# Attention scores with tokens on partitions, and the exponentials turned by block transposes and copies in SBUF

## The chip, the cores and the metric

The kernel runs on one core of one Trainium2 chip. A core has five engines that run side by side, each in its own program order: TensorE (PE, with its weight loads as PEld), VectorE (DVE), ScalarE (ACT), GpSimd (POOL) and SyncE (SP), which here only issues copies. Copies run on 16 DMA engines, fed by queues; a copy issued by SP waits in SP's queue until what it depends on is done, and the copies behind it wait with it. SBUF holds tiles of 128 partitions; PSUM has eight banks of 128 x 512 numbers of 32 bits, into which TensorE writes.

The metric is device time in microseconds (us) for one execution, lower being better.

## The reference

One transformer block over 2048 tokens of width 576. A conditioning vector gives six rows (shift, scale, gate for each half). The first half is attention: 32 query heads over 16 cached key and value heads, with the last 512 keys only and no mask. The second half is a gated ReLU network of width 4608.

```python
W = min(4096, max(256, Sk // 4))                      # 512
q = (x @ wq).reshape(B, Sq, Hq, Dh).transpose(0, 2, 1, 3)
k = jnp.repeat(k_cache[:, :, Sk - W:, :], rep, axis=1)
v = jnp.repeat(v_cache[:, :, Sk - W:, :], rep, axis=1)
scores = jnp.einsum("bhqd,bhkd->bhqk", q, k) * (Dh ** -0.5)
p = softmax(scores, axis=-1)
o = jnp.einsum("bhqk,bhkd->bhqd", p, v)
return o.transpose(0, 2, 1, 3).reshape(B, Sq, Hq * Dh) @ wo
...
h = layernorm(x) * (1 + ca) + sa
x = x + ga * A(h)
h = layernorm(x) * (1 + cb) + sb
x = x + gb * B(h)            # B: (relu(h @ W_gate) * (h @ W_up)) @ W_down
```

## The kernel before

**Numbers in two parts.** TensorE multiplies in a format (F32R) that keeps only part of a 32-bit number. So each operand is split into a high part, a copy in that format (`hi`, made by ScalarE), and a low part, the rest (`lo`, a subtraction on POOL or VectorE). A product is three matmuls: high by high, and the two mixed ones.

**Units.** Attention runs over 128 units; a unit is one head and one block of 512 tokens. Two heads share a key and value head. The loop at the end of the program issues, for each unit u, the scores of u, the projection of the queries of u+1 (`qproj`, 14 matmuls of 512 columns), the values of u-1 (12 matmuls) and two pieces of the output projection (`wo_piece`, 12 matmuls of 288 columns each, adding to the running output `acc`). `run(u, k)` puts further steps at hooks between them: weights to load and split, layer norms, the rearranging of the second half's weights. The order on PE, VectorE, ScalarE and POOL is that of the program text; nothing is reordered afterwards.

**A unit before.** The scores lie with keys on partitions: in `s_half` the keys are the stationary operand, the 512 tokens the moving one (12 matmuls, two halves of 128 x 1024 numbers in PSUM, pool `psS` with two buffers). The maximum over the keys is thus across partitions. It is found by transposing reductions on VectorE (L546), a small reduction (L551), a transpose of 32 x 32 blocks (`turn`, L562), a transpose on TensorE (`spread`, L565) and another reduction (L585), and laid out over the partitions by a transpose of a broadcast (L589). `exp_half` subtracts it on VectorE (L602, PSUM to SBUF) and takes the exponential on ScalarE (L604, 128 x 1024). The sum for the denominator is made like the maximum: additions on VectorE and POOL (`ksum_op`, L619, L622), then L556 and the second half of the small transposes; for the first three units (`by_sum`) TensorE sums with a matrix of ones (`pv_sums`). `hi_half` (L597) and `lo_half` (L611) split the exponentials at the end of unit u; `pv_half` uses them in unit u+1, the first half before and the second half after the exponentials of that unit. `o_mul` (L668) divides by the sum, `o_hi` and `o_lo` split the result.

**Output pieces before.** For most pieces ScalarE copies `acc` into PSUM first (`put_seed`, L720), the matmuls add to it, and ScalarE copies it back (L696); the others are added by VectorE (L698).

**Tiles.** `pp` holds exponentials, high and low parts (three, three and two buffers of 128 x 1024); `psM` has two PSUM buffers of one bank, for projections, small transposes and values in turn; `psW` has one of two banks for the output pieces.

Of the kernel before, what the change touches and what calls it, by code (L numbers as in the profile page):

```python
# [26 lines left out]
SUM, MLP0 = 3, 8  # L27
# [4 lines left out]
def kernel(  # L32
# [22 lines left out]
    pp = ctx.enter_context(tc.tile_pool(name="pp", bufs=3))  # L55
# [4 lines left out]
    sp = ctx.enter_context(tc.tile_pool(name="sp", bufs=2))  # L60
    psS_scope = tc.tile_pool(name="psS", bufs=2, space=bass.MemoryType.PSUM, side="right")
# [17 lines left out]
    mxs = cp.tile([P, 32], F32, name="mxs")  # L79
    nc.vector.memset(mxs, 0.0)  # L80

    zeros = cp.tile([P, 32], F32, name="zeros")
    nc.vector.memset(zeros, 0.0)

    onesr = cp.tile([P, P], F32R, name="onesr")
    nc.vector.tensor_copy(onesr, ones)
# [146 lines left out]
    def prep_kv(d, g, j):  # L233
        st = {}

        def load():
            st["raw"] = rp.tile([P, 640], F32, tag="raw", name=f"rkv{g}_{j}")
            nc.sync.dma_start(st["raw"][:, :512], kv[g, j])

        def cut():  # L240
            d[g] = wp.tile([P, 10, P], F32R, tag="wB", name=f"kv{g}_{j}")
            split(st["raw"][:, :512].rearrange("p (t n) -> p t n", t=4), 512,
                  d[g][:, 0:4, :], d[g][:, 4:8, :])

        return load, cut
# [51 lines left out]
    pend, pend_act = [], []  # L297
# [3 lines left out]
    def flush(q=None):  # L301
        q = pend if q is None else q
        while q:
            q.pop()()

    class LayerNorm:
# [51 lines left out]
        def norm(self, i, by_pool=()):  # L358
            pool, tag, w = self.where[i]
            n = pool.tile([P, w], F32, tag=tag, name=f"xn{self.key}_{self.qb}_{i}",  # L360
                          **({"bufs": 2} if tag == "lo" else {}))
# [18 lines left out]
        def trans(self, ds, pool, tag, tiles=range(4)):  # L380
            nm = f"lt{self.key}_{self.qb}_{ds[0]}"
            if tag == "w":
                flush()
                flush(pend_act)
# [13 lines left out]
        def affine(self, ds, pool, tag, engs):  # L398
# [26 lines left out]
            for j, (d, e) in enumerate(zip(ds, engs)):  # L425
                nm = f"lf{self.key}_{qb}_{d}"
                if len(e) > 3:
                    fs[d] = self.ps[d]
                elif tag == "p":
                    fs[d] = pool.tile([P, 1024], F32, tag="hi" if d % 2 else "p", name=nm)[:, :512]  # L430
                else:
                    fs[d] = pool.tile([P, 512], F32, tag=tag, name=nm)
# [93 lines left out]
    st_, t4, mt, pt, hi_, lo_, bc, rb, rinv, ks_, pvps, done, o, bps = ({} for _ in range(14))  # L526

    def by_sum(u):
        return 0 <= u < SUM

    sums_ps = {}

    def s_half(u, h):
        g, qb, hd = unit(u)
        k = ks[g]
        t = psS.tile([P, 2, 512], F32, tag="s", name=f"s{u}_{h}")
        st_[u, h] = t
        for j in range(2):
            kt = 2 * h + j
            ps = t[:, j, :]  # L540
            nc.tensor.matmul(ps, k[:, kt, :], qhi[u], start=True, stop=False)  # L541
            nc.tensor.matmul(ps, k[:, 4 + kt, :], qhi[u], start=False, stop=False)  # L542
            nc.tensor.matmul(ps, k[:, kt, :], qlo[u], start=False, stop=True)  # L543
        if h == 0:
            t4[u] = sp.tile([P, 4, 16], F32, tag="t4", name=f"t4_{u}", bufs=1)
        nc.vector.tensor_reduce(t4[u][:, 2 * h:2 * h + 2, :].rearrange("p k b -> p (k b)"),  # L546
                                t.rearrange("p k (b j) -> p (k b) j", j=32),
                                axis=AX.X, op=ALU.max, apply_transpose=True)

    def max_pre(u):  # L550
        nc.vector.tensor_reduce(mxs[:, :16], t4.pop(u).rearrange("p k b -> p b k"), axis=AX.X, op=ALU.max)  # L551

    def sum_pre(u):
        if by_sum(u):
            return
        nc.vector.tensor_reduce(mxs[:, 16:], ks_.pop(u).rearrange("p (b j) -> p b j", j=32),  # L556
                                axis=AX.X, op=ALU.add, apply_transpose=True)

    def turn(u):
        bps[u] = psM.tile([P, 512], F32, tag="mm", name=f"qm{u}")  # L560
        mt[u] = sp.tile([P, P], F32, tag="mt", name=f"mt{u}", bufs=1)
        nc.vector.transpose(mt[u].rearrange("p (a b) -> p a b", a=4), mxs[:, None, :].to_broadcast([P, 4, 32]))  # L562

    def spread(u):
        nc.tensor.transpose(bps[u][:, :P], mt.pop(u), ident)  # L565

    def quads(u, k):
        return bps[u][:, :P].rearrange("p (a k b) -> p k b a", a=4, k=2)[:, k]

    def sum_add(u):  # L570
        r = rinv[u] = sp.tile([P, 16], F32, tag="ri", name=f"ri{u}", bufs=1)
        nc.vector.tensor_reduce(r, quads(u + 1, 1), axis=AX.X, op=ALU.add)

    def sum_inv(u):
        nc.vector.reciprocal(rinv[u], rinv[u])

    def sum_bc(u):
        r = rinv.pop(u)
        rb[u] = bp.tile([P, 512], F32, tag="bc", name=f"rb{u}")
        nc.vector.transpose(rb[u].rearrange("p (b j) -> p b j", j=32),  # L580
                            r[:, :, None].to_broadcast([P, 16, 32]))

    def max_bc(u):
        r = sp.tile([P, 16], F32, tag="r", name=f"r{u}", bufs=1)
        nc.vector.tensor_reduce(r, quads(u, 0), axis=AX.X, op=ALU.max)  # L585
        if u > SUM:
            sum_add(u - 1)
        m = bp.tile([P, 512], F32, tag="bc", name=f"mb{u}")
        nc.vector.transpose(m.rearrange("p (b j) -> p b j", j=32),  # L589
                            r[:, :, None].to_broadcast([P, 16, 32]))  # L590
        if u > SUM:
            sum_inv(u - 1)
        bc[u] = m

    def hi_half(u, h):
        hi_[u, h] = pp.tile([P, 2, 512], F32R, tag="hi", name=f"hi{u}_{h}")
        nc.scalar.copy(hi_[u, h], pt[u, h])  # L597

    def exp_half(u, h):
        t = st_.pop((u, h))  # L600
        p = pp.tile([P, 2, 512], F32, tag="p", name=f"p{u}_{h}")
        nc.vector.tensor_tensor(p, t, bc[u][:, None, :].to_broadcast([P, 2, 512]),  # L602
                                op=ALU.subtract)
        nc.scalar.activation(p, p, AF.Exp, bias=0.0, scale=1.0)  # L604
        pt[u, h] = p
        if h == 0 and u:
            hi_half(u, 0)

    def lo_half(u, h):
        lo_[u, h] = pp.tile([P, 2, 512], F32R, tag="lo", name=f"lo{u}_{h}", bufs=2)  # L610
        nc.gpsimd.tensor_sub(lo_[u, h], pt[u, h], hi_[u, h].bitcast(F32))  # L611

    def ksum_op(u, h):
        if by_sum(u):
            return
        p = pt[u, h]
        if h == 0:
            ks_[u] = xp.tile([P, 512], F32, tag="xm", name=f"ks{u}")
            nc.vector.tensor_tensor(ks_[u], p[:, 0, :], p[:, 1, :], op=ALU.add)  # L619
        else:  # L620
            for j in range(2):
                nc.gpsimd.tensor_tensor(ks_[u], ks_[u], p[:, j, :], op=ALU.add)  # L622

    def pv_half(u, h, late=False):
        g, qb, hd = unit(u)
        if h == 0:
            pvps[u] = psM.tile([P, 512], F32, tag="mm", name=f"pv{u}")
        ps, v, a, b = pvps[u], vs[g], hi_[u, h], lo_[u, h]
        for j in range(2):
# [1267 lines left out]
```

## Time and profile before

| | |
|---|---|
| runs shown | 2839.78, 2840.68, 2841.32 us |
| median | 2840.68 us |
| span of the profiled execution, first to last instruction | 2839.2 us |
| mean granted TensorE clock in it | 1.000 |
| DVE, ACT, POOL busy in 1000 to 1200 us | 164.99, 132.44, 173.91 us of 200 |
| mean DMA rate over the span | 145 GB/s |

The time of the profiled execution is its span and a little around it: the median stands 1.5 us over the span. Attention fills the first 1.6 thousand of the 2839 us; the gated network fills the rest.

How to read the profile's rows. A group of instructions reads: line of the program, engine, operation, tile written <- tiles read, shapes, count | busy time in us, mean ns of one | idle time of the engine just before them <- what ended most of it. A row of the timeline reads: start in us, time taken in us, engine, line, operation, tiles, shapes, count, and in brackets the idle time before it with what ended it. A busy PE is pipelined: the next matmul starts before the one before has ended. The chain that ended last follows the work back from the last instruction, at each step to what released it.

### The profile page before, as it was taken

Reading aid. Unit: us, or ns where it says so; the run is one execution under the profiler, and the core shown is the slowest. Engines: PE = TensorE matmul, PEld = TensorE weight load, DVE = VectorE, ACT = ScalarE, POOL = GpSimd, SP = SyncE. Lnnn points to the kernel's source line nnn. Section 1 sums busy time; section 2 is a strip of 40 time slices with the busy share of each in tenths; the row PEclk is TensorE's granted clock in tenths of the full one; section 3 lists DMA queues with packets and bytes.
Section 4 is the critical chain, followed back from the end, with each engine's and each line's share of the span. In section 5 each row is a group of like instructions: output and inputs, shape, how many; then the busy total and the mean of one; then the engine's idle time right before and its main releaser. Section 6 shows DMA issues by size and latency. Waiting matters only on the chain.

```text
span 2839.2 us, 41692 instructions
## 1 busy us (share of the span) xinstructions
PE 2823.0 (99%) x15183; PEld 2457.3 (87%) x15183; DVE 2194.6 (77%) x3220; ACT 1431.0 (50%) x2020; POOL 2206.1 (78%) x1596
## 2 busy tenths in 40 slices
PE   9999999999999999999999999999999999999999
PEld 7888888888888888888888888888888888888888
DVE  8988788888888888777988877787787566666666
ACT  6766666676666666666756433333333222222220
POOL 6878888888898988777788766778888577777773
PEclk9999999999999999999999999999999999999999
DMA  6322122223332223322244465666677844444443
GB/s 248 109 76 97 60 94 95 84 70 109 106 96 85 93 67 132 100 69 86 73 144 136 149 219 203 228 228 232 248 254 281 313 154 155 156 156 154 152 149 136
DMA packets 166876, 411.40 MB, mean 145 GB/s; under 512 B 15728, under 2 KB 62576, under 8 KB 166672
## 3 DMA queue, kind: packets, MB, share of 16 engines
q1 hardware_dynamic: 132768, 287.65, 31.4%
q10 hardware_dynamic: 33904, 121.09, 10.9%
q8 instruction: 120, 1.97, 0.3%
q14 instruction: 84, 0.69, 0.1%
HBM read 276.53 MB, written 160.73 MB: 154 GB/s over the span
## 4 chain that ended last, share of the span: by engine, by line
PE 90%; POOL 4%; DVE 2%; ACT 2%; issue 1%; DMA 1%; ACTq 0%; SPq 0%; POOLq 0%; DVEq 0%
PE gh_P L1163 28%; PE wo L687 12%; PE qps L465 12%; PE md L687 9%; PE mf L771 6%; PE s L543 4%; PE s L542 4%; PE s L541 3%; PE pv L634 3%; PE pv L632 3%; PE pv L631 3%; POOL lo L611 2%; PE gu L1163 1%; POOL ks L622 1%; ACT p L604 1%
## 5 line engine op out<-in xcount | busy, mean ns | idle before, releaser
L611 POOL TENSOR_TENSOR lo<-p,hi 128x1024 fp32r<-128x1024 f32 x256 | 610.1, 2405 | 0.5
L622 POOL TENSOR_TENSOR ks<-ks,p 128x512 f32<-128x512 f32 x250 | 334.5, 1338 | 247.5 <-ACT p L604 203.4
L546 DVE TRANSPOSE_TENSOR_REDUCE t<-s 128x32 f32<-128x1024 f32 x256 | 317.6, 1245 | 137.9 <-PE s L543 125.6
L1163 PE MATMUL gh_P<-hop_B,wop 128*128 128x512 f32 x1470 | 352.9, 390 | 0.6 <-issue 0.6
L1163 PEld LDWEIGHTS gh_P<-hop_B,wop 128*128 128x128 f32 x1470 | 270.0, 188 | 51.2 <-DVE q L1200 0.8
L602 DVE TENSOR_TENSOR p<-s,mb 128x1024 f32<-128x1024 f32 x256 | 299.9, 1209 | 0.3
L465 PE MATMUL qps<-hTa,wA 128*128 128x512 f32 x1176 | 282.6, 391 | 0.7 <-DVE hTa L447 0.3
L1163 PE MATMUL gh_P<-hop_T,wop 128*128 128x512 f32 x1138 | 282.8, 390 | 0.0
L687 PE MATMUL wo<-woga,ohi 128*128 128x288 f32 x1344 | 279.1, 300 | 1.0 <-POOL woga L217 0.5
L604 ACT ACTIVATE p<-p 128x1024 f32<-128x1024 f32 x256 | 270.4, 1056 | 17.4 <-DVE p L602 17.4
L597 ACT CAST hi<-p 128x1024 fp32r<-128x1024 f32 x256 | 268.9, 1051 | 6.9
L465 PEld LDWEIGHTS qps<-hTa,wA 128*128 128x128 f32 x1176 | 220.1, 188 | 47.9 <-DVE hTa L447 0.8
L687 PE MATMUL md<-wogb,hhi 128*128 128x288 f32 x1280 | 257.2, 294 | 0.0
L519 ACT ACTIVATE qhi<-qps 128x512 fp32r<-128x512 f32 x128 | 76.6, 598 | 337.2 <-PE qps L465 337.2
L1163 PEld LDWEIGHTS gh_P<-hop_T,wop 128*128 128x128 f32 x1138 | 208.8, 188 | 39.3
L687 PEld LDWEIGHTS wo<-woga,ohi 128*128 128x128 f32 x1344 | 218.7, 188 | 16.2 <-ACT p L604 0.8
L687 PEld LDWEIGHTS md<-wogb,hhi 128*128 128x128 f32 x1280 | 212.3, 188 | 10.5 <-DVE q L1188 0.2
L698 DVE TENSOR_TENSOR acc<-md,acc 128x576 f32<-128x576 f32 x160 | 120.0, 754 | 107.2 <-PE md L687 106.1
L1163 PE MATMUL gh_P<-hy_T,wop 128*128 128x512 f32 x618 | 200.6, 391 | 0.0
L687 PE MATMUL wo<-woga,olo 128*128 128x288 f32 x672 | 198.8, 296 | 1.2 <-POOL olo L676 1.1
L687 PE MATMUL md<-wogb,hlo 128*128 128x288 f32 x640 | 188.8, 295 | 0.0
L696 ACT COPY acc<-wo 128x576 f32<-128x576 f32 x228 | 145.0, 636 | 55.1 <-PE wo L687 50.5
(322 smaller groups left out, 7279.7 us busy)
## 6 DMA issues: line engine op xcount, KB each, us to landing
wop<-wk_P SPq DMA_DIRECT2D x133, 640.0 KB
wk_P<-wop ACTq DMA_DIRECT2D x119, 640.0 KB
wr<-wlay SPq DMA_DIRECT2D x68, 384.0 KB
againq<-akq SPq DMA_DIRECT2D x22, 640.0 KB
againo<-ako SPq DMA_DIRECT2D x18, 576.0 KB
rogb<-wd SPq DMA_DIRECT2D x36, 288.0 KB
rwA<-wq SPq DMA_DIRECT2D x32, 320.0 KB
roga<-wo SPq DMA_DIRECT2D x32, 288.0 KB
```

Source lines behind the costliest of these rows:

```text
L465: return [lambda i=i, a=a, b=b: nc.tensor.matmul(ps, a, b, start=(i == 0), stop=(i == n - 1)) for i, (a, b) in enumerate(ops)]
L546: nc.vector.tensor_reduce(t4[u][:, 2 * h:2 * h + 2, :].rearrange("p k b -> p (k b)"), t.rearrange("p k (b j) -> p (k b) j", j=32), axis=AX ...
L597: nc.scalar.copy(hi_[u, h], pt[u, h])
L602: nc.vector.tensor_tensor(p, t, bc[u][:, None, :].to_broadcast([P, 2, 512]), op=ALU.subtract)
L604: nc.scalar.activation(p, p, AF.Exp, bias=0.0, scale=1.0)
L611: nc.gpsimd.tensor_sub(lo_[u, h], pt[u, h], hi_[u, h].bitcast(F32))
L622: nc.gpsimd.tensor_tensor(ks_[u], ks_[u], p[:, j, :], op=ALU.add)
L687: nc.tensor.matmul(ps[:, half, :H2], a[:, sl], w[b][:, cs], start=(n == 0 and seed is None), stop=(n == 5), skip_group_check=seed is not None)
L696: nc.scalar.copy(av, ps[:, :, :H2])
L698: nc.vector.tensor_tensor(av, ps[:, :, :H2], av, op=ALU.add)
L771: nc.tensor.matmul(ps[:, j, :H2], x[:, sl], w[:, c:c + H2], start=i == 0, stop=i == 2)
L1163: nc.tensor.matmul(ps, a, c, start=s not in ("P2", "P3") and i == 0, stop=i == len(ops) - 1, skip_group_check=True)
```

## The change

The scores are laid out the other way, tokens on partitions: in `s_half` a slice of 128 tokens is the stationary operand and the 512 keys the moving one. The matmuls are as many and as large. The maximum is then along a row: one reduction per half, with the sign turned. `exp_half` takes four exponentials of 128 x 512 on ScalarE, in place in PSUM, with the turned maximum as a bias of each partition, and gets the sum of each row as a second output.

The value matmuls still need keys on partitions. So `turn_half` transposes blocks of 32 x 32 on VectorE out of PSUM into one tile in SBUF (`T`, one buffer), and `send` moves the blocks between partitions by 16 copies of 32 partitions x 2 KB on SP's queue, into `PT` (two buffers). The keys are loaded in an order that makes these runs contiguous. The row of reciprocal sums goes out to DRAM in pieces of 4 bytes (`sum_row`) and comes back broadcast over the partitions (`sum_bc`).

`hi_half` and `lo_half` of unit u-1 stand behind the exponentials of unit u, and the low part is written over the exponentials themselves in `PT`. Both halves of the values of u-1 stand at the end of unit u, behind both output pieces. `o_mul` moves to the start of the unit after, with its operands in another order of columns. All output pieces are added by VectorE; the second one of a unit takes a buffer of the scores' pool. The transposes on TensorE, the sums by TensorE in the first units, the additions for the sum and the seeding of pieces are gone. The second half of the program takes its buffers from pools (`pl`, `pp`) that are opened once those of attention are closed.

```diff
-            split(st["raw"][:, :512].rearrange("p (t n) -> p t n", t=4), 512,
-                  d[g][:, 0:4, :], d[g][:, 4:8, :])
+            if j:
+                split(raw.rearrange("p (t n) -> p t n", t=4), 512, hi, lo)
+            else:
+                split(raw.rearrange("p (k c n) -> p c k n", k=4, c=4), 512,
+                      *(x.rearrange("p c (k n) -> p c k n", k=4) for x in (hi, lo)))
...
     def s_half(u, h):
+        k = ks[unit(u)[0]]
+        khi, klo = (k[:, x:x + 4, :].rearrange("p t n -> p (t n)") for x in (0, 4))
+        t = st_[u, h] = psS.tile([P, 2, 512], F32, tag="s", name=f"s{u}_{h}")
+        for j in range(2):
+            ps, sl = t[:, j, :], slice((2 * h + j) * P, (2 * h + j + 1) * P)
+            nc.tensor.matmul(ps, qhi[u][:, sl], khi, start=True, stop=False)
+            nc.tensor.matmul(ps, qhi[u][:, sl], klo, start=False, stop=False)
+            nc.tensor.matmul(ps, qlo[u][:, sl], khi, start=False, stop=True)
+        if h == 0:
+            nm[u] = sp.tile([P, 4], F32, tag="nm", name=f"nm{u}")
+            sm[u] = sp.tile([P, 4], F32, tag="sm", name=f"sm{u}")
+        nc.vector.tensor_reduce(nm[u][:, 2 * h:2 * h + 2], t, axis=AX.X, op=ALU.max, negate=True)
+
+    def exp_half(u, h):
+        t = st_[u, h]
+        for j in range(2):
+            i = 2 * h + j
+            nc.scalar.activation(t[:, j, :], t[:, j, :], AF.Exp, bias=nm[u][:, i:i + 1], scale=1.0,
+                                 accum_out=sm[u][:, i:i + 1])
+
+    def turn_half(u, h):
+        if h == 0:
+            tt[u] = tp.tile([P, 4, 4, 4, 32], F32, tag="T", name=f"T{u}")
+        nc.vector.transpose(tt[u][:, :, :, 2 * h:2 * h + 2, :].rearrange("p c k j t -> p j (c k) t"),
+                            st_.pop((u, h)).rearrange("p j (b t) -> p j b t", t=32))
+
+    def send(u):
+        t = tt.pop(u)
+        pt[u] = pa.tile([P, 4, 4, P], F32, tag="PT", name=f"PT{u}")
+        for a in range(4):
+            for c in range(4):
+                nc.sync.dma_start(pt[u][32 * c:32 * c + 32, a].rearrange("p k n -> p (k n)"),
+                                  t[32 * a:32 * a + 32, c].rearrange("p k i t -> p (k i t)"))
+
+    def sum_row(u):
+        r = sp.tile([P, 4], F32, tag="rr", name=f"r{u}")
+        nc.vector.reciprocal(r, sm.pop(u))
+        nc.sync.dma_start(rrow[u].rearrange("i p -> p i"), r)
+
+    def sum_bc(u):
+        rb[u] = bp.tile([P, 512], F32, tag="bc", name=f"rb{u}")
+        nc.sync.dma_start(rb[u], rrow[u].rearrange("i p -> (i p)")[None, :].to_broadcast([P, 512]))
+
+    def part(t, h):
+        return t[:, :, 2 * h:2 * h + 2, :].rearrange("p a k n -> p k a n")
+
+    def hi_half(u, h):
+        hi_[u, h] = pa.tile([P, 2, 4, P], F32R, tag="hi", name=f"hi{u}_{h}")
+        nc.scalar.copy(hi_[u, h], part(pt[u], h))
+
+    def lo_half(u, h):
+        nc.gpsimd.tensor_sub(part(pt[u].bitcast(F32R), h), part(pt[u], h), hi_[u, h].bitcast(F32))
+
+    def pv_half(u, h):
...
+            hi = a[:, j].rearrange("p a n -> p (a n)")
+            nc.tensor.matmul(ps, v[:, kt, :], hi, start=(kt == 0), stop=False)
+            nc.tensor.matmul(ps, v[:, 4 + kt, :], hi, start=False, stop=False)
+            nc.tensor.matmul(ps, v[:, kt, :], b[:, :, kt, :], start=False, stop=(kt == 3))
...
     def o_mul(u):
         o[u] = rb.pop(u)
-        nc.vector.tensor_tensor(o[u], done.pop(u), o[u], op=ALU.mult)
+        t = o[u].rearrange("p (i a t) -> p a i t", i=4, a=4)
+        nc.vector.tensor_tensor(t, done.pop(u).rearrange("p (a i t) -> p a i t", a=4, i=4), t, op=ALU.mult)
```

The order within a unit, after the change:

```python
    for u in range(NU):
        last = u + 1 == NU
        run(u, 0)
        if u > 1:
            o_mul(u - 2)
        s_half(u, 0)
        s_half(u, 1)
        if u > 1:
            o_hi(u - 2)
            o_lo(u - 2)
        if u:
            sum_bc(u - 1)
        run(u, 1)
        if not last:
            qproj(u + 1, 0, 14)
        run(u, 2)
        exp_half(u, 0)
        turn_half(u, 0)
        exp_half(u, 1)
        turn_half(u, 1)
        send(u)
        sum_row(u)
        if u > 1:
            hi_half(u - 1, 0)
            lo_half(u - 1, 0)
        if not last:
            q_hi(u + 1)
            q_lo(u + 1)
...
        if u:
            hi_half(u - 1, 1)
            lo_half(u - 1, 1)
        run(u, 3)
        todo = pieces(u)
        if todo:
            pend.append(wo_piece(*todo[0]))
        run(u, 4)
        run(u, 5)
        flush()
        run(u, 6)
...
        if todo:
            pend.append(wo_piece(*todo[1], pool=(psS, "s")))
        run(u, 7)
        if u:
            pv_half(u - 1, 0)
            pv_half(u - 1, 1)
        flush()
        run(u, 8)
        run(u, 9)
```

More of the change, by code (lines that the diff above doesn't have):

```diff
@@ L538, in s_half @@
+    def pv_half(u, h):
+        if h == 0:
+            pvps[u] = psM.tile([P, 512], F32, tag="mm", name=f"pv{u}")
+        ps, v, a, b = pvps[u], vs[unit(u)[0]], hi_.pop((u, h)), pt[u].bitcast(F32R)
         for j in range(2):
             kt = 2 * h + j
[L540 to L543, printed above, removed]
@@ L559, in turn @@
[L559 to L572, printed above, removed]
@@ L609, in lo_half @@
[L609 to L622, printed above, removed]
@@ L1807 @@
[L1807 to L1826 removed]
+        run(u, 2)
```

301 lines of the change are left out of this document (75 added, 226 removed).

## The prediction

> **What bounds the kernel now.** I read the page first: its head, part 1 (busy time) and part 4 (the chain that ended last).
>
> ```profile
> span 2839.2 us, 41692 instructions
> PE 2823.0 (99%) x15183; PEld 2457.3 (87%) x15183; DVE 2194.6 (77%) x3220; ACT 1431.0 (50%) x2020; POOL 2206.1 (78%) x1596
> PE 90%; POOL 4%; DVE 2%; ACT 2%; issue 1%; DMA 1%; ACTq 0%; SPq 0%; POOLq 0%; DVEq 0%
> ```
>
> TensorE (PE) bounds it, and the others have slack only on average. So the question is not how much work leaves VectorE (DVE) and GpSimd (POOL), but whether the operands still reach TensorE in time within one unit. For that I read the timeline: first score matmul of the first unit, of three neighbours, and the other TensorE groups of a unit; the "wo" group as the chain in order of time shows it.
>
> ```profile
> 23.61 0.50 PE L541 MATMUL s<-qhi,kv 128*128 128x512 f32 x1 [0.69 <-ACT qhi L519]
> ...
> 985.06 0.39 PE L541 MATMUL s<-qhi,kv 128*128 128x512 f32 x1
> ...
> 997.03 0.39 PE L541 MATMUL s<-qhi,kv 128*128 128x512 f32 x1
> ...
> 999.77 3.35 PE L465 MATMUL qps<-hTa,wA 128*128 128x512 f32 x14
> 1002.95 0.27 PE L565 MATMUL qm<-ident,mt 128*128 128x128 f32 x1
> ...
> 1008.98 0.39 PE L541 MATMUL s<-qhi,kv 128*128 128x512 f32 x1
> ...
> 1568.27 0.39 PE L541 MATMUL s<-qhi,againk 128*128 128x512 f32 x1
> 991.26 1.59 PE wo L687 x12
> ```
>
> The first column is the start, the second the time taken. A unit takes 11.97 and 11.95 us here, and the 127 steps from 23.61 to 1568.27 average 12.163. Fourteen matmuls of 512 take 3.35 us, the last of them 0.39, so one is issued every (3.35 - 0.39)/13 = 0.228 us. TensorE's own work per unit is 12 scores + 14 projections + 12 values = 38 x 0.228 = 8.66, and two pieces of 1.59: 11.84 us. The remaining 0.1 is the small transpose L565. So attention has no gap to win, except that transpose.
>
> **The change, part by part: what leaves TensorE.** L565 goes: 0.1 us x 128 = 13 us at most. The three first units lose 8 sum matmuls each: 24 x 0.228 = 5.5 us. Scores, projections, values and pieces keep their counts and sizes. If nothing waits, that is 18 us less.
>
> **What TensorE must wait for.** Before, hi and lo of unit u are made at the end of unit u. After, both are put behind the four exponentials of unit u+1 in ScalarE's (ACT) queue, and TensorE uses them at the end of the same unit u+1. Engines run in order, so a path from the scores of one unit, through the queues, to the values of the unit before now lies inside one unit. Its rows, from the page's groups and the groups by shape, and two POOL instructions on end in the timeline:
>
> ```profile
> L546 DVE TRANSPOSE_TENSOR_REDUCE t<-s 128x32 f32<-128x1024 f32 x256 | 317.6, 1245 | 137.9 <-PE s L543 125.6
> L597 ACT CAST hi<-p 128x1024 fp32r<-128x1024 f32 x256 | 268.9, 1051 | 6.9
> L519 ACT ACTIVATE qhi<-qps 128x512 fp32r<-128x512 f32 x128 | 76.6, 598 | 337.2 <-PE qps L465 337.2
> L439 ACT ACTIVATE lta<-lta,mcol,mcol 128x512 f32<-128x512 f32 x5 | 3.7, 749 | 3.0 <-PE lta L395 2.1 <-DVE t L546 0.9
> L101 ACT ACTIVATE sT<-cT 128x5 f32<-128x5 f32 x1 | 0.2, 209 | 0.4 <-DMA cT<-c 0.4
> L611 POOL TENSOR_TENSOR lo<-p,hi 128x1024 fp32r<-128x1024 f32 x256 | 610.1, 2405 | 0.5
> 1571.38 4.76 POOL L611 TENSOR_TENSOR lo<-p,hi 128x1024 fp32r<-128x1024 f32 x2
> 1014.91 0.27 PE L565 MATMUL qm<-ident,mt 128*128 128x128 f32 x1
> 1015.22 0.22 DVE L585 TENSOR_REDUCE r<-qm 128x16 f32<-128x64 f32 x1 [0.77 <-PE qm L565]
> ```
>
> One hand-over costs 1015.22 - 1015.18 = 0.04 us. Zero is the first score matmul:
> - scores of the first half end: 5 x 0.228 + 0.39 = 1.53
> - maximum: 0.04 + 1.245 (nearest row L546, same source) = 2.82
> - four exponentials of 512 elements, e us each: 2.86 + 4e
> - hi of the first half of the unit before, behind them: + 1.05 (L597)
> - two lo on POOL: 0.04 + 4.76
> - TensorE needs the second lo at its fourth matmul from the end: 0.04 + 4 x 0.228 = 0.95, then the next unit begins.
>
> The sum is 9.66 + 4e. TensorE itself would reach that matmul 11.84 - 0.91 = 10.93 into the unit; it waits wherever 4e is over 2.2 us.
>
> The trace has no exponential of 512 with a per-partition bias, in place in PSUM, with a sum as second output. L519 (598 ns, constants only) bounds it below: two instructions on end overlap, so a pitch of about 0.6. L439 (749 ns, in place in PSUM, two per-partition operands) is the nearest row; if the sum takes an instruction of its own as small as L101 (209 ns), the end is 0.96. I take 0.78, next to L439, since the sum's output must cost something and one pointer less something back. The period is then 12.78 us. With 0.6 the second maximum decides instead (scores 2.90, maximum to 4.19, two exponentials to 5.43): 12.23. With 0.96 it is 13.50.
>
> The Trainium skill, "ScalarE: Activation LUTs", section "What ACT_TABLE_LOAD costs", gives about 280 ns + 0.833 ns per element with a pointer bias and an overlap of about 93 ns on end. Its constants-only form, 186 ns + 0.833 ns, comes to 0.61 us where L519 has 0.598, so the trace agrees there. The estimate for one exponential on end is then 0.61 us and the period 12.23, which still waits; the section prices no sum output, and no run here shows one yet.
>
> **The sum.** The first nine units (139.32 - 23.61 = 115.7 us by the tenth start, below) hold start-up and norms; without pieces their TensorE work is short and the path counts there too: 9.8 + 8 x 12.78 + some 6 for norms = 118, so +2.
>
> ```profile
> 139.32 0.39 PE L541 MATMUL s<-qhi,againk 128*128 128x512 f32 x1
> L376 ACT ACTIVATE xna<-acc,rsa 128x512 f32<-128x512 f32 x8 | 6.5, 806 | 0.0
> L376 ACT ACTIVATE xta<-acc,rsa 128x128 f32<-128x128 f32 x6 | 2.9, 482 | 0.0
> ```
>
> The other 118 steps take 127 x 12.163 - 115.7 = 1429 us now, 19 of them extra TensorE work, which the wait would swallow. After: 118 x 12.78 = 1508, so +79. In a dozen units norm work (0.81 + 0.48 us per tile) stands in ScalarE's queue ahead of the exponentials, with only some 1.3 us of idle time (from o's high part, done near 1.5, to 2.86) to hide it; I put down 15 us, between 0 and 30. At the end the last values wait for the copies and for both lo with little else to issue: +4 (0 to 10). Together 79 + 2 + 15 + 4 = +100. The runs shown have a median of 2840.68, 1.5 over the profiled span: 2839.2 + 1.5 + 100 = **2941 us**.
>
> **What costs nothing, and its cover.** VectorE gains two maxima, two transposes and two additions (mostly ScalarE copies before), and loses both subtractions, three small transposes, the add for the sum and the reductions. POOL loses two sum additions. Both end with less work, so only order counts. The turn of the first half ends near 2.86 + 1.56 + 0.04 + 1.25 = 5.7; a second piece takes that score buffer at 7.5: 1.8 us of cover. One transpose should lie between L580 (0.70 for half the size) and L546 (1.245), two between 1.4 and 2.5; off the path at either end. Behind ACT's added wait stand q's high part (done near 7.6, wanted by the next scores at 12.8) and the second hi (8.6, wanted by POOL at 9.4); behind POOL's lo stand weight lows and o's low part, wanted by a piece six us into the next unit. Strided reads in hi, lo and the value matmuls, lo in place and the permuted multiply I take at their rows before; a tenth more or less on the lo pair alone moves the period by 0.5 us, and no row excludes it.
>
> Copies: 16 per unit on SyncE's queue (SP), then the two for the row of sums (512 pieces of 4 bytes out, a broadcast row back, used one unit later: a unit of cover), with the weight loads queued behind the first one's wait for the turn.
>
> ```profile
> L580 DVE STREAM_TRANSPOSE rb<-ri x128: 699/701/712, 47.0 to 1594.0; 128x512 f32<-128x512 f32 x128
> 1428.15 0.81 SPq L486 DMA_DIRECT2D againo<-ako  x2
> 1429.06 0.38 SPq L881 DMA_DIRECT2D hk_B<-hy_B  x1
> 350.56 0.58 SPq L1573 DMA_DIRECT2D wlay<-wg  x1
> 1007.00 0.34 SPq L254 DMA_DIRECT2D roga<-wo  x1
> 1008.70 1.56 DVE L262 TENSOR_TENSOR roga<-roga,mrow 128x576 f32<-128x576 f32 x1
> ```
>
> An issue takes 0.4 us on end; a load issued at 1007.00 was used at 1008.70, so 1.7 us to landing at most. The single turned tile is busy for 2.5 (two turns) + 16 x 0.4 + 1.7 = 10.6 us, under the period, and the turned copy lands some 3 us before its hi. The loads behind have a unit of lead. So nothing, as long as an issue stays under 0.53 us.
>
> **The rivals.**
> - *No wait, and faster.* The path must come in under 11.84. It decides at 4e = 2.2 and a second maximum that doesn't bind, or a lo pair 0.4 us cheaper than 4.76. Then only TensorE's relief is left: 2841 - 18 = 2823. Against it: even the cheapest exponential gives 12.23.
> - *The turned tile binds.* At the 0.58 us that a DRAM-to-DRAM copy (L1573) takes to issue, the tile's loop is 2.5 + 9.3 + 1.7 = 13.5: +164 + 21, 3026. For it: the queue is also held by waiting loads; against: the sends are plain copies.
> - *Lo in place holds its neighbour.* If the two halves, interleaved in one tile, are ordered as if they overlapped, hi of the second half waits for the first lo (9.45), the second lo ends at 13.0, and ten value matmuls follow: 15.3 per unit, +376 + 20, 3237. No row shows halves interleaved like this.
>
> **How the numbers follow.** Chances: the path as summed 0.70 (2876 at e = 0.6, as 118 x 12.23 - 1429 + 21 = +35; 3026 at 0.96), turned tile 0.10, lo in place 0.07, no wait 0.09, within 0.2% 0.04. About 0.2%, 6 us, is what a measurement can tell from no change. The range, 2845 to 3060, takes the first case with both ends of e, a little beyond for norms and tail, and most of the second; left out are the faster case and the 3237. Faster 0.09, same 0.04, slower 0.87.
>
> **What would show it.** Right: TensorE idle 0.5 to 1.5 us in each unit ahead of a values matmul that reads lo, released by POOL lo; score starts 12.2 to 13.5 us apart; POOL idle until ACT hi, ACT's hi directly behind the exponentials; DVE and POOL less busy. Wrong: starts 11.85 apart; or VectorE's transposes waiting for a DMA (turned tile); or ACT's second hi waiting for POOL lo (in place). The exponential's mean time tells the size of e.

## The result, and the profile after

The changed kernel takes 4377.10 us (median; 4372.76 to 4379.74) where the kernel before takes 2840.83 (2839.78 to 2841.32): a ratio of 1.541 (1.539 to 1.543), +1536 us. The forecast was slower, but by 100 us, and the time lies far outside its range. First the page of the changed kernel: span, busy time, the chain that ended last by engine and by line, and the packets.

```profile
span 4375.8 us, 44794 instructions
PE 3171.4 (72%) x15030; PEld 2722.4 (62%) x15030; DVE 1933.5 (44%) x2427; ACT 1270.2 (29%) x2332; POOL 1872.9 (43%) x1346
DMA packets 351221, 579.79 MB, mean 132 GB/s; under 512 B 118128, under 2 KB 164976, under 8 KB 350992
DMA 44%; PE 31%; SPq 20%; issue 2%; POOL 1%; ACT 1%; DVE 0%; ACTq 0%; DVEq 0%; POOLq 0%
DMA rr<-r 20%; SPq L566 18%; PE gh_P L1064 18%; DMA rb<-rr 9%; PE md L624 6%; DMA wlay<-wu 5%; DMA wlay<-wg 4%; PE mf L672 4%; DMA PT<-T 1%; POOL PT L586 1%; PE wo L624 1%; DMA againq<-akq 1%; SPq L240 1%; DMA akq<-wA 1%; DMA againo<-ako 1%
```

Every compute engine has slack, TensorE too. The chain, 90% TensorE before, is now 44% DMA and 20% SyncE's queue (SPq). Its lines are the row of sums written to DRAM (rr<-r), the issue of the sixteen copies (L566), the row read back (rb<-rr), and two transfers that the change did not touch: wlay<-wu and wlay<-wg, which lay out the gate and up weights anew in DRAM. Then the waits (waiting engine and line, what it waited for; total us, times, longest), with SyncE's own queue last.

```profile
PE wo L624 <- DVE T L558: 897.4, 120, 23.0
DVE rb L605 <- DMA rb<-rr: 842.4, 109, 14.1
DVE T L558 <- DMA PT<-T: 560.7, 101, 13.2
ACT hi L583 <- DMA PT<-T: 414.7, 110, 26.4
SPq L576 <- DMA rr<-r: 796.9, 114, 9.8
```

TensorE waits for a score buffer (wo piece, L624), VectorE's turn holds that buffer, and the turn waits for the copies of the turn before. So the single turned tile binds, the rival to which I gave 0.10, and with far longer copies than it assumed. The timeline of SyncE's queue shows two units (start, time taken, line, transfer, count).

```profile
1499.83 0.53 SPq L572 DMA_DIRECT2D rr<-r  x1
1500.40 0.64 SPq L1467 DMA_DIRECT2D wlay<-wu  x1
1501.14 4.30 SPq L261 DMA_DIRECT2D roga<-wo  x1
1510.89 0.33 SPq L576 DMA_DIRECT2D rb<-rr  x1
1511.27 0.62 SPq L1467 DMA_DIRECT2D wlay<-wu  x1
1511.98 18.36 SPq L566 DMA_DIRECT2D PT<-T  x16
1530.44 0.53 SPq L572 DMA_DIRECT2D rr<-r  x1
1531.02 0.53 SPq L980 DMA_DIRECT2D wa_P<-wlay  x1
1531.59 0.66 SPq L1467 DMA_DIRECT2D wlay<-wg  x1
1532.35 9.79 SPq L261 DMA_DIRECT2D roga<-wo  x1
1542.23 0.46 SPq L576 DMA_DIRECT2D rb<-rr  x1
```

The unit is the queue: 30.6 us from the row of 1499.83 to that of 1530.44, a long one. A weight load (roga<-wo) that issues in 0.34 us in the kernel before takes 4.30 and 9.79 behind the row; the read-back (L576) begins 11 us after the row's write; the sixteen copies take 18.36 us. Attention runs from the first to the last of these score matmuls of a unit:

```profile
24.31 0.50 PE L540 MATMUL s<-kv,qhi 128*128 128x512 f32 x1 [0.69 <-ACT qhi L523]
3066.96 0.39 PE L540 MATMUL s<-againk,qhi 128*128 128x512 f32 x1
```

That is 3042.7 us, 24.0 per step, against 1544.7 before (23.61 to 1568.27): +1498 of the +1536. The rest lies behind the last unit.

### The profile page after: what moved, and what is told of

It reads as the page before. It is cut to its first block, busy times and chain, and to the rows that moved or that the text cites. A ratio compares the mean times of both kernels' runs of the same rounds, so it can differ in the third digit from the quotient of the medians.

```text
span 4375.8 us, 44794 instructions
## 1 busy us (share of the span) xinstructions
PE 3171.4 (72%) x15030; PEld 2722.4 (62%) x15030; DVE 1933.5 (44%) x2427; ACT 1270.2 (29%) x2332; POOL 1872.9 (43%) x1346
## 2 busy tenths in 40 slices
DMA packets 351221, 579.79 MB, mean 132 GB/s; under 512 B 118128, under 2 KB 164976, under 8 KB 350992
## 4 chain that ended last, share of the span: by engine, by line
DMA 44%; PE 31%; SPq 20%; issue 2%; POOL 1%; ACT 1%; DVE 0%; ACTq 0%; DVEq 0%; POOLq 0%
DMA rr<-r 20%; SPq L566 18%; PE gh_P L1064 18%; DMA rb<-rr 9%; PE md L624 6%; DMA wlay<-wu 5%; DMA wlay<-wg 4%; PE mf L672 4%; DMA PT<-T 1%; POOL PT L586 1%; PE wo L624 1%; DMA againq<-akq 1%; SPq L240 1%; DMA akq<-wA 1%; DMA againo<-ako 1%
## 5 line engine op out<-in xcount | busy, mean ns | idle before, releaser
L586 POOL TENSOR_TENSOR PT<-PT,hi 128x1024 fp32r<-128x1024 f32 x256 | 604.1, 2382 | 913.8 <-ACT hi L583 902.8
L624 PE MATMUL wo<-woga,ohi 128*128 128x288 f32 x1344 | 392.0, 388 | 736.6 <-DVE T L558 631.4
L624 PEld LDWEIGHTS wo<-woga,ohi 128*128 128x128 f32 x1344 | 303.7, 262 | 773.2 <-DVE T L558 652.4
L558 DVE STREAM_TRANSPOSE T<-s 128x1024 f32<-128x1024 f32 x256 | 305.0, 1229 | 725.6 <-DMA PT<-T 560.7
L613 POOL TENSOR_TENSOR olo<-rb,ohi 128x512 fp32r<-128x512 f32 x128 | 162.6, 1270 | 612.6 <-ACT ohi L609 609.8
L583 ACT CAST hi<-PT 128x1024 fp32r<-128x1024 f32 x256 | 266.1, 1041 | 447.5 <-DMA PT<-T 414.7
L624 PE MATMUL wo<-againo,ohi 128*128 128x288 f32 x576 | 165.0, 382 | 305.3 <-DVE T L558 266.0
L552 ACT ACTIVATE s<-s,nm 128x512 f32<-128x512 f32 x512 | 337.4, 659 | 76.0 <-DVE nm L546 64.9
L609 ACT CAST ohi<-rb 128x512 fp32r<-128x512 f32 x128 | 79.1, 618 | 897.2 <-DVE rb L605 897.2
L624 PEld LDWEIGHTS wo<-againo,ohi 128*128 128x128 f32 x576 | 127.0, 256 | 322.5 <-DVE T L558 275.7
L546 DVE TENSOR_REDUCE nm<-s 128x2 f32<-128x1024 f32 x256 | 301.1, 1215 | 13.6 <-PE s L542 13.6
L624 PE MATMUL wo<-woga,olo 128*128 128x288 f32 x672 | 256.7, 382 | 21.9 <-POOL olo L613 21.9
L624 PE MATMUL md<-wogb,hhi 128*128 128x288 f32 x1280 | 257.2, 295 | 0.0
L630 DVE TENSOR_TENSOR acc<-wo,acc 128x576 f32<-128x576 f32 x256 | 191.3, 750 | 111.6 <-PE wo L624 111.5
L624 PEld LDWEIGHTS md<-wogb,hhi 128*128 128x128 f32 x1280 | 212.3, 188 | 10.5 <-DVE q L1089 0.2
```

The lines of the kernel that those rows point to most:

```text
L546: nc.vector.tensor_reduce(nm[u][:, 2 * h:2 * h + 2], t, axis=AX.X, op=ALU.max, negate=True)
L552: nc.scalar.activation(t[:, j, :], t[:, j, :], AF.Exp, bias=nm[u][:, i:i + 1], scale=1.0, accum_out=sm[u][:, i:i + 1])
L558: nc.vector.transpose(tt[u][:, :, :, 2 * h:2 * h + 2, :].rearrange("p c k j t -> p j (c k) t"), st_.pop((u, h)).rearrange("p j (b t) -> p ...
L583: nc.scalar.copy(hi_[u, h], part(pt[u], h))
L586: nc.gpsimd.tensor_sub(part(pt[u].bitcast(F32R), h), part(pt[u], h), hi_[u, h].bitcast(F32))
L613: nc.gpsimd.tensor_sub(olo[u], o.pop(u), ohi[u].bitcast(F32))
```

## The experiments

Each kernel ran beside the kernel before on the same chip (2839.7 to 2840.3 us), with one profile and one time. The effects are tens to hundreds of microseconds. "Sends" are the sixteen copies of a unit.

### Taking the row of sums away, or its pieces

**row_once** writes the row for the first unit only and lets every unit read that one back.

```diff
-        nc.sync.dma_start(rrow[u].rearrange("i p -> p i"), r)
+        if u == 0:
+            nc.sync.dma_start(rrow[0].rearrange("i p -> p i"), r)
```

> The row of reciprocal sums is written to DRAM for the first unit only and every unit reads that one back, so the denominators are left out of the result from the second unit on; the 16 copies, the broadcast and all orders stay. Theory (SyncE's queue is the loop): the row's 512 pieces of 4 bytes hold the queue and the rings for some 10 us a unit (issued at 1499.83, its reader released at 1510.89); without them the loop is two turns 2.4 + 16 issues of 0.63 + about 2 to landing = 14.5 us a unit in place of 22.4: about 128 x 7.9 = 1010 us less, 3370. Rival (the path from scores to the low part, as forecast, is what fills the unit): nothing of it is touched, 4377. Rival (moving 1 MB between partitions is what is slow): sends stay as long as they are, 18 us a unit, about 4000 or more.

Measured 3480.12 us, 897 less than the changed kernel and 110 above the theory's 3370. The pages count the pieces; this one's row of packets:

```profile
DMA packets 284162, 579.49 MB, mean 167 GB/s; under 512 B 51072, under 2 KB 97920, under 8 KB 283936
```

118128 - 51072 = 67056 packets fewer, 127 rows of 528 (512 pieces and 16 that I take for the completion signals), with 0.3 MB between them. So the row costs by its number of pieces or by the wait of its reader, not by bytes. I held that it is the reader (L576), which waits at the head of SyncE's queue with the sends behind it; the rival was the pieces. **bc_late** moves the reader behind the sends:

```diff
-        if u:
-            sum_bc(u - 1)
         run(u, 1)
...
         send(u)
+        if u:
+            sum_bc(u - 1)
         sum_row(u)
```

> The read-back of the row of unit u-1 is issued behind the 16 copies of unit u, not ahead of them; nothing is left out. Theory (the copies stand in the queue behind a wait for the row): the wait is over by then, so 14.5 to 16 us a unit, 3350 to 3560. Rival (the pieces stall the DMA rings themselves, whoever waits): the copies' issue stays blocked, over 20 us a unit, 4100 or more.

4305.07 us: only 72 less. The reader's wait was the longest in the queue's list, 797 us, and moving it explains next to nothing: it still comes to 363 us here, and the queue stalls all the same. My theory of that moment fell. **row16** keeps row and reader, but writes 128 pieces of 16 bytes:

```diff
-        nc.sync.dma_start(rrow[u].rearrange("i p -> p i"), r)
+        nc.sync.dma_start(rrow[u], r)
```

> The whole change with the right result, but the row of sums goes to DRAM as 128 pieces of 16 bytes instead of 512 pieces of 4 bytes; the permutation is done where the output is multiplied (the output's two halves then come from PSUM by ScalarE and VectorE). If the number of pieces sets the stall of the queue (512 pieces about 10 us behind them, 128 about 2.5 us), the unit falls to about 17.5 to 19 us, 3550 to 3730 us, near the 3480 of row_once. Rival: the stall belongs to a write and a dependent read through DRAM as such, whatever the pieces: it stays at 22 us per unit, 4250 to 4400.

3606.92 us, 770 less, with nothing left out. The same edit makes o's high part (ScalarE) and low part (now VectorE) straight from the product in PSUM, and what that alone costs was not run. A quarter of the pieces leaves 3607 - 3480 = 127 of the 897 us, so the pieces are the cost. **before_plus_row** adds the write alone, without a reader, to the kernel before:

```diff
         turn(u)
+        nc.sync.dma_start(xrow[u].rearrange("i p -> p i"), mhalf)
```

> The kernel before, with the same DRAM write of 512 pieces of 4 bytes added to SyncE's queue once a unit and nobody reading it. If the pieces stall whatever comes behind them in the DMA rings for 10 us, weight loads come late and the time rises: by 50 to 500 us. If only a waiting reader makes them dear, the time stays within 10 us of 2841.

3142.88 us, +302: the pieces alone slow a kernel that doesn't use them, 2.4 us per row on average. Nothing holds these writes to one per unit, so the queue runs ahead of the units. In one place it issues eighteen on end, and ScalarE, which issues copies on a queue of its own, stands idle for 33 us:

```profile
1312.63 50.75 SPq L1778 DMA_DIRECT2D xr<-mhalf  x18
1351.84 1.04 ACT L597 CAST hi<-p 128x1024 fp32r<-128x1024 f32 x1 [33.12 <-DMA xr<-mhalf]
```

Two steps there take 42 and 59 us and lose 77 between them, a quarter of the 302. The last row is issued at 1424.6 us, and the last 37 steps take as long as in the kernel before.

**norm** needs no row: VectorE multiplies the exponentials by the reciprocal sums in PSUM, ahead of the turn.

```diff
+        nc.vector.reciprocal(r, sm[u][:, 2 * h:2 * h + 2])
+        nc.vector.tensor_tensor(st_[u, h], st_[u, h], r[:, :, None].to_broadcast([P, 2, 512]), op=ALU.mult)
```

> Nothing is left out: VectorE multiplies the exponentials in PSUM by the reciprocal sums before the turn (two multiplications of 128 x 1024, about 1.2 us each), so no row goes through DRAM, and o is split from PSUM (the low part on VectorE). Theory (the queue is the loop): as without the row's pieces, 14.5 us a unit plus up to 2.4 for the multiplications inside the turned tile's loop or its queue: 3370 to 3680. Rival (path of the forecast): 12.8 to 13.5 a unit, 3060 to 3150. Rival (data of the copies): about 4000.

3540.07 us, 837 less than the changed kernel, with nothing left out.

### The path alone

**path_only** is row_once with the sends of the first two units only; later units read those two tiles again. All compute instructions and their order stay.

```diff
+        if u > 1:
+            pt[u] = pts[u % 2]
+            return
```

> Leaves out: the row of sums of all units but the first, and the copies of the turned tile of all units but the first two; later units read the two tiles of the first two again (their turned data is not computed with). All of TensorE's, VectorE's, ScalarE's and GpSimd's instructions and their order stay. So only the forecast path is left: scores, maximum, four exponentials, hi, lo, values. Theory (the path inside a unit was summed rightly and DMA alone made the rest): score starts 12.8 us apart, as forecast with e = 0.78, about 2940 us, between 2876 (12.23) and 3026 (13.50). Rival (the engines' queues hold more than that path: lo in place, the strided reads, a second maximum): 14 us or more per unit, 3090 or over. If it is at 11.9 per unit, 2823, no path binds at all.

3020.63 us. One unit in the timeline, TensorE's, ScalarE's and GpSimd's rows together:

```profile
1453.50 0.61 PE L540 MATMUL s<-againk,qhi 128*128 128x512 f32 x1
1465.53 0.50 PE L601 MATMUL pv<-PT,againv 128*128 128x512 f32 x1 [0.68 <-POOL PT L590]
1466.57 0.40 PE L540 MATMUL s<-againk,qhi 128*128 128x512 f32 x1
1469.47 0.66 ACT L552 ACTIVATE s<-s,nm 128x512 f32<-128x512 f32 x1 [1.30 <-DVE nm L546]
1470.05 0.19 ACT L552 ACTIVATION_READ_ACCUMULATOR s<-s,nm 128x1 f32 x1
1472.34 0.19 ACT L552 ACTIVATION_READ_ACCUMULATOR s<-s,nm 128x1 f32 x1
1472.44 1.04 ACT L587 CAST hi<-PT 128x1024 fp32r<-128x1024 f32 x1
1473.55 4.75 POOL L590 TENSOR_TENSOR PT<-PT,hi 128x1024 fp32r<-128x1024 f32 x2 [4.01 <-ACT hi L587]
1473.86 1.05 ACT L587 CAST hi<-PT 128x1024 fp32r<-128x1024 f32 x1
24.33 0.50 PE L540 MATMUL s<-kv,qhi 128*128 128x512 f32 x1 [0.69 <-ACT qhi L523]
191.74 0.40 PE L540 MATMUL s<-againk,qhi 128*128 128x512 f32 x1
1740.75 0.40 PE L540 MATMUL s<-againk,qhi 128*128 128x512 f32 x1
```

From 1466.57 the first exponential starts 2.90 us in (forecast 2.86), hi 5.87 (5.98), lo 6.98 (7.07), and TensorE's wait for lo stands where it was forecast, ahead of a values matmul that reads lo (L601). The median of the 127 steps is 12.83 us; 12.78 was forecast. The last three rows of the fence start the first, the tenth and the last unit. **path_hi_first** moves hi and lo of the first half ahead of the exponentials:

```diff
+        if u > 1:
+            hi_half(u - 1, 0)
+            lo_half(u - 1, 0)
         exp_half(u, 0)
```

> path_only (3021 us; leaves out the copies after the second unit and the rows after the first) with hi and lo of the first half of the unit before put ahead of the four exponentials instead of behind them. If the order in ScalarE's queue makes the 12.83 us of path_only, the first lo starts at 2.6 us instead of 7 and the second ends near 10.1, ahead of the 10.93 at which TensorE wants it: 11.85 to 12.0 us per unit, 2870 to 2920 us. Rival (lo on GpSimd is late because of its other work, weight lows and o's low part, whatever the order): 12.5 or more, 2980 or over.

2898.56 us. Two neighbouring units of it:

```profile
1208.86 0.40 PE L540 MATMUL s<-againk,qhi 128*128 128x512 f32 x1
1220.76 0.40 PE L540 MATMUL s<-againk,qhi 128*128 128x512 f32 x1
```

11.90 us, TensorE's own pace. The order on ScalarE's queue made the 12.83 us. Of the 58 us that are left over the kernel before, 48 lie in the first nine steps (163.5 us against 115.7), where the copies of two units and one row still run; the other 118 steps take 5 us more than before. So 2899 is no floor of this order, and where it would stand without any copy isn't shown.

### What the sends cost

**row_once_split** is row_once with every second send issued from ScalarE's queue, behind its hi.

```diff
-                nc.sync.dma_start(pt[u][32 * c:32 * c + 32, a]...
+                if c % 2 != act:
+                    continue
+                (nc.scalar if act else nc.sync).dma_start(pt[u][32 * c:32 * c + 32, a]...
```

> Leaves out the row of sums of all units but the first, as row_once does (3480 us, median unit 15.8 us), and issues the 16 copies from two queues: eight from SyncE where they were, eight from ScalarE behind its hi of the same unit. Theory: what the copies cost is the loop of the single turned tile, two turns 2.5 us, sixteen issues of 0.63 us, 2 us to landing, 14.6 us, and with eight issues per queue it is 9.5 us, under the path; so the unit falls to the path's 12.8 to 13.3 us, 3010 to 3100 us, near path_only's 3021, which has no copies at all. Rival (the copies cost by the traffic that they bring, or by the wait for their landing): 15 us or more per unit, 3350 or over.

3343.47 us: between the theory and the rival. Its trace has the hint: units of 16.8 us on average as long as layout copies (wlay) still leave the queue, and runs of units of 12.8 after the last of them (median there 13.4). So two kernels leave out 132 of those 152 copies:

```diff
+        if i >= len(lay0):
+            continue
         step("lay", ...
```

**split_nolay** on two queues, **one_nolay** on one.

> row_once_split (3343 us, leaves out the row of sums after the first unit) without the copies that lay out the gate and up weights anew in DRAM (132 of the 152 on SyncE's queue during attention, 512-byte packets; their readers take the first two blocks instead, so the gate and up weights of the later feature tiles are not the right ones). If those copies and the sends hold each other on SyncE's queue, the units up to the 88th fall from 16.8 us to those after it, 12.8 to 13.3: 3000 to 3080 us, near path_only's 3021. Rival (the sends themselves are slow while any load runs): 15 us or more per unit, 3250 or over.

> row_once (3480 us, 16 sends on one queue) without the same layout copies. Then the loop of the single turned tile is left: two turns 2.5 us, 16 issues of 0.63 us = 10.1, 2.0 to landing, 14.6 us per unit, as row_once has it after its 88th unit: 118 units of 1.8 us over the path's 12.83 more than path_only's 3021, 3190 to 3260 us. If it is near split_nolay, the issue of the sends is not the bound; if it stays above 3350, other loads hold the queue too.

3049.51 us on two queues, and 3259.51 on one, at the upper end of its range. Now the loop of the turned tile is seen bare; first one_nolay, VectorE's turns and SyncE's sends:

```profile
1011.65 2.38 DVE L558 STREAM_TRANSPOSE T<-s 128x1024 f32<-128x1024 f32 x2 [4.20 <-DMA PT<-T]
1014.09 10.02 SPq L566 DMA_DIRECT2D PT<-T  x16
1025.73 2.38 DVE L558 STREAM_TRANSPOSE T<-s 128x1024 f32<-128x1024 f32 x2 [2.56 <-DMA PT<-T]
L566 SPq DMA_DIRECT2D PT<-T x2048: 507/588/2181, 36.2 to 1992.8; - x187
```

2.44 us from the turns' start to the first issue, 10.02 of issues, 1.62 to landing: 14.08 us in this unit, 14.85 as the median of all steps, above the path's 12.83. Then split_nolay, where SyncE and ScalarE issue side by side:

```profile
1009.20 4.96 SPq L569 DMA_DIRECT2D PT<-T  x8
1009.76 5.36 ACTq L569 DMA_DIRECT2D PT<-T  x7
1014.69 0.40 PE L540 MATMUL s<-kv,qhi 128*128 128x512 f32 x1
1027.52 0.39 PE L540 MATMUL s<-kv,qhi 128*128 128x512 f32 x1
```

Half the issues per queue, and the unit is back on the path: 12.83. The Trainium skill, "DMA: Bandwidth & Descriptors", section "Issuing engines are not separate DMA queues", says that a second issuing engine saves only the sequencer's time to initiate, usually small beside the transfer. The trace agrees on what is saved and not on its size: here the issue is 10.02 us and the landing 1.62, and the second queue saves 3259.5 - 3049.5 = 210 us.

### Versions meant to mend the change

These leave nothing out. **norm_split2** is norm on two queues; **norm_via** is norm with the turned tile written to DRAM in one DMA and read back in four; **row16_split** is row16 on two queues; **row16_split_hi** has hi first as well.

> The kernel norm (VectorE normalises the exponentials, no row through DRAM) with the 16 copies of the turned tile issued from two queues: eight from SyncE where they were, eight from ScalarE behind its hi of the same unit. Theory: the single turned tile's loop (turns and multiplications 3.7 to 5 us, 16 issues of 0.63 us = 10 us, landing 2 us) is the unit of norm (median 16.5 us); with eight issues per queue it falls to 11 to 12 us, so the forecast path binds: 12.8 to 14 us per unit, 2945 to 3100 us. Rival: the copies are limited by what the DMA rings can take of them, not by the issuing queue: still 16 to 17 us per unit, 3500.

> The kernel norm with the move between partitions made through DRAM: the turned tile is written out in one DMA (512 packets of 2048 bytes) and read back in four, five issues instead of sixteen. Theory (the number of issues on SyncE's queue prices the copies): the turned tile is busy for 4 to 5 us of turns, under 1 us of issue and 4 to 5 us of writing, under 11 us, so the unit falls to 12.8 to 14 us, 2945 to 3100 us. Rival (bytes or the landing of 1 MB each way price them): 16 us or more per unit, 3450 or over.

> The whole change, both causes mended as far as they go: the row of sums in 128 pieces of 16 bytes, and the copies on two queues, with the right result. Theory: SyncE's queue then holds 8 issues (5 us), a stall of about 2.5 us and loads of 2 us, 9.5 us, under the path of 12.8, so 12.9 to 13.8 us per unit, 3020 to 3150 us. Rival: the rings stay full behind the pieces on either queue: 15 us or more, 3350 or over.

> row16_split, whole and with the right result, with hi and lo of the first half of the unit before ahead of the exponentials. The turned copy must land by about 1.5 us into the next unit for that: the turn ends near 8, ScalarE issues its eight by 13 to 14, they land by 15 to 16, 3 us into the next unit, so hi first makes the exponentials wait 1 to 2 us for the copy: 12.5 to 13.5 us per unit, 2960 to 3100 us. If the copies land in time, 11.9 to 12.2 and 2880 to 2940. If worse than row16_split, the landing of the copies has become the wait.

Measured 3441.98, 3430.19, 3491.57 and 3539.35 us: all four missed on the slow side. In norm_split2 VectorE's turn waits little for the copies (58 us in all, 459 in row_once); two neighbouring units show a longer path instead:

```profile
1510.41 2.35 DVE L545 TENSOR_REDUCE nm<-s 128x2 f32<-128x1024 f32 x2
1513.54 1.23 DVE L557 TENSOR_TENSOR s<-s,r 128x1024 f32<-128x1024 f32 x1
1514.81 1.25 DVE L560 STREAM_TRANSPOSE T<-s 128x1024 f32<-128x1024 f32 x1
1517.40 1.25 DVE L560 STREAM_TRANSPOSE T<-s 128x1024 f32<-128x1024 f32 x1
1518.68 5.01 ACTq L571 DMA_DIRECT2D PT<-T  x8
1521.96 0.39 PE L599 MATMUL pv<-PT,kv 128*128 128x512 f32 x1
1525.31 0.58 ACT L607 CAST ohi<-pv 128x512 fp32r<-128x512 f32 x1
1525.92 0.69 DVE L609 TENSOR_TENSOR olo<-pv,ohi 128x512 fp32r<-128x512 f32 x1 [5.37 <-ACT ohi L607]
1526.53 2.35 DVE L545 TENSOR_REDUCE nm<-s 128x2 f32<-128x1024 f32 x2
```

From maximum to maximum 16.12 us. The first turn ends at 1516.06, behind its reciprocal and multiplication (1.4 us), and only then is the score buffer free for a piece on TensorE, behind which stand the values and the next scores. The next maximum stands on VectorE behind o's low part (L609), which waits 5.37 us for o's high part on ScalarE (L607). The values end at 1522.35, but ScalarE makes the high part only at 1525.31, because the eight sends that it now issues, two other issues and two copies stand ahead of it. Over all units it starts 2.8 us after the values (median). So the second queue frees SyncE and lengthens the path through ScalarE. In norm_via the read from DRAM lands too late for hi (a wait of ScalarE on it of 349.5 us in all). In row16_split the layout copies were still there, and a median step near 13.9 us behind the last of them, down from 18.3 on average, says that they are part of it. VectorE also waits 374 us in all for the row's read-back (rb<-rr); how the rest divides was not tried. Hi first (row16_split_hi) loses 48 us against row16_split, and ScalarE's hi now waits 258 us in all for DMA. The profile puts that wait down to the row's write (rr<-r), which is issued right behind the sends and which hi doesn't read, so that the landing of the sends has become the wait is my reading. No version tried beats the kernel before.

## Why the prediction was wrong, point by point

**Where the 1536 us lie.** By what was taken away, in this order: path_only stands 180 us above the kernel before; the sends on one queue add 239 (one_nolay, 3260); the layout copies in that queue 221 (row_once, 3480); the row of sums 897 (4377). The parts depend on one another, so another order would divide them otherwise. The step of 239 is not a clean one: path_only still has the layout copies and one_nolay doesn't.

**What bounds the kernel and what leaves TensorE** was right: where nothing waits, path_hi_first runs at 11.90 us per unit, and 11.84 was forecast.

**The path inside a unit** was right in mechanism and size: 12.83 us against 12.78. The exponential's e, taken as 0.78, comes to (1472.44 - 1469.47)/4 = 0.74 here. It is an activation of 0.66 and a read of the sum of 0.19, the guess behind the upper bound; the two overlap a little, which keeps it under 0.78. That the sum is off by 0.05 only is partly luck: the four exponentials came out 0.15 us under, and hand-overs, maximum and the end of the path 0.2 over.

**Start-up and norms** were too small. In path_only the first nine steps (24.33 to 191.74) take 167 us, not 115.7 + 2: +52 where the forecast had +2, part of it the DMAs that this kernel still has in its first units (the second to the fourth step take 74.5 us, 38.6 before). The other 118 take 1549 instead of 1508 + 15, and the tail adds 7 where 4 was forecast. So the path with all its ends is worth 180 at most, not 100: inside the range (3021 against 3060); the 80 us too few are 6% of the miss.

**The copies at nothing** was the first step that failed. "An issue takes 0.4 us on end" came from loads of DRAM into SBUF; a copy from SBUF to SBUF takes 0.59 and follows the next by 0.63. My own bound, nothing as long as an issue stays under 0.53 us, was thus crossed. The rival that I priced at 0.58 us (13.5 per unit, 3026) is the right mechanism, and 14.08 to 14.85 is what it measured bare. The nearest row, a DRAM-to-DRAM copy of 0.58, stood in the prediction itself; I called the sends "plain copies" and gave it 0.10.

**"The loads behind have a unit of lead"** was the second. I asked whether the loads could wait for the sends, and not whether the sends could wait for the loads: 132 layout copies share the queue and cost the turned tile 221 us.

**The row of sums with "a unit of cover"** was the third, and the largest. Cover was counted for its reader; the row's price falls on the copies that come behind it. "512 pieces of 4 bytes" stood in the prediction as a description and carried no price, and no rival had it. The Trainium skill, "DMA: Bandwidth & Descriptors", section "Rules for kernel authors", says that a transfer whose last dimension isn't contiguous becomes one descriptor per element; the packet count above agrees, and row_once and row16 give the price.

**The rivals.** No wait fell: TensorE waits for lo even without any copy. Lo in place fell: path_only has both halves in place, and the two lo follow each other in 4.75 us, and hi of the second half (1473.86) runs beside the first lo instead of waiting for it.

## What to carry to other kernels

Price a moved step on its queue, not only on its engine: for every DMA that a change adds, count issues and pieces, take the issue time from a row of the same kind (SBUF to SBUF is not DRAM to SBUF), and ask who stands behind it in that queue and, where the pieces are small, in the others. Cover for a transfer's reader is no cover for its neighbours. A wait that tops the list can be a symptom: moving the reader took away 72 us, removing the pieces 897.

## What the hardware showed that I had not expected

- 512 pieces of 4 bytes, 2 KB in all, take 11 us from the row's write to the read-back behind it (1499.83 to 1510.89). Three stretches of time: most of that wait, the time behind it, and the eighteen rows on end in before_plus_row:

```profile
1503.00:1511.00 8.00, 8.00 (x35) 7.02 (x35) 2.77 (x5) 1.21 (x2) 5.32 (x3) 0.82 0.99 45
1513.00:1524.00 11.00, 4.27 (x17) 3.12 (x16) 3.62 (x4) 3.78 (x9) 2.63 (x2) 0.80 0.34 101
1321.00:1351.00 30.00, 4.55 (x21) 3.48 (x19) 7.61 (x12) 0.00 (x0) 3.77 (x3) 0.65 1.31 1
```

  The columns end with granted clock, DMA share (packet time over that of the sixteen engines; packets can overlap, so it can pass 1) and GB/s. In the third stretch the trace's packet records show nothing but 4-byte pieces, and the engines are full with them at 1 GB/s. So it is the small pieces themselves that fill the engines. In the first stretch the pieces have started by 1502, and the engines are full (0.99) at 45 GB/s with the packets behind them, those of ScalarE's queue too: its packets of 5 KB take 1.24 us on average (6.9 at most) in the time from 1 to 9 us behind a row's issue, and 0.23 at other times in attention. A row thus slows copies on both queues, and not only those behind it in SyncE's.
- Between 1513 and 1524 the sends stand still, by the chain for a layout copy issued at 1511.27, while the engines are a third busy (0.34). So it isn't bandwidth that runs out there. What it is, a limit on what may be outstanding or something else in the queue, these runs don't tell.
- The granted clock of TensorE was lower where it idled: 0.80 in the second of those stretches, against 1.00 in path_only from 400 to 1700 us, where TensorE waits about 1 us per unit. A wo matmul of 288 columns took 388 ns (L624) in the changed kernel and 300 (L687) before. I read it as a consequence of the waits; no run sets the clock apart from them.
- The layout copies, which had run in the kernel before without anyone noticing, became a bound as soon as something urgent was put behind them.
